# First backward heads of an attention block's gradient kernel: Wo products by batch with sums on TensorE, broadcasts moved, dV halves between V products

## Chip, cores and metric

The kernel runs on one core of one Trainium2 chip. The metric is the device time in microseconds, the median of three runs. Engines are named as in the profile: PE (TensorE), DVE (VectorE), ACT (ScalarE), POOL (GpSimd), SP (SyncE, which here only issues DMAs). PEld is PE's load of the stationary operand.

## The reference, cut to what matters

One decode step (one query row) through an adaLN-modulated attention block with a K/V cache and an MLP block, and its gradient.

```python
q = (x @ wq).reshape(B, Sq, Hq, Dh)              # Hq = 32 heads, Dh = 192
scores = einsum('bhqd,bhkd->bhqk', q, k_cache) * Dh ** -0.5   # 8192 keys
p = softmax(scores)
o = einsum('bhqk,bhkd->bhqd', p, v_cache)
a = o.reshape(B, Sq, Hq * Dh) @ wo               # wo: 6144 x 640
...
_out, _vjp = jax.vjp(_f, A_x, A_k_cache, A_v_cache, A_wq, A_wo, B_w3, B_w4, c, w_mod)
_grads = _vjp(grad_out)
```

All arrays are bf16. The large outputs are the gradients of the two caches, each 32 x 8192 x 192. For one head, with dao the gradient of `a` (640 numbers): `do = wo_h . dao` (192 numbers), `dP = V . do` and `dV = p x do` for each key, `dS = p * (dP - c)` with `c = do . o`, and `dK = dS x q`, an outer product as dV is.

## The kernel before

**Tiling.** A head's K or V is 128 partitions x 64 keys x 192. It is handled in two halves of 32 keys per partition ([128, 32, 192] in bf16, 1536 KB). A forward pass goes over heads 0 to 31, the MLP and its gradient follow, and a backward pass goes over heads 31 to 0 (`HS`; step `i` works on head 31 - i). V is loaded again for the backward pass; of K only head 31's tiles are read there (`dq_last`), still in place.

**One backward step i**, for head `h` and the next head `nxt`:
- `bwd_mult(h, t)` for both halves: DVE multiplies V by do in place (L132), PE sums the 192 products of each key by 24 matmuls with an identity (L1004) into a PSUM bank of 64 x 8 columns, `dP_ps`. The V slot is then free.
- `bwd_pf(nxt)`: p of the next head, on ACT as f32 (`PF`), on DVE as pairs in bf16 (`P2h`).
- `bwd_dv(nxt, t)`: an outer product of p and do in a store buffer; 20 of the 32 keys by ACT (L1009, one instruction per key), 12 by one DVE instruction (L987), then the store on SP's queue (L1012).
- `hook(i)` for the first ten steps (below).
- jobs that go with the step (rows of dWo and others, by ACT, stored from POOL's queue).
- `bwd_ds(h)`: DVE sums dP's 8 columns (L1030) and forms dS. For head 31, `dq_last` follows: 128 matmuls of K with dS.
- `bwd_dk(h, t)`: two outer products on DVE (L987), each stored on SP's queue (L1039).

Engines run in the order in which the program is written (`pin_order` ties PE, DVE and ACT to it), and SP's queue issues in that order too: a DMA whose condition is not met holds those behind it.

**Buffers.** dV and dK share a few tiles of 1536 KB (`big_tile`; tags 0 to 4 in a fixed order), so an outer product waits until an earlier store from its tile has landed. V has six slots. `ring_load` issues the next loads of a fixed list (`ring`) as far as the slot's last content is in `freed`; V loads go to SP's queue. The list also has Wo's rows in batches of two or three head pairs (`BATCHES`), loaded by `load_wo` from POOL's queue into one such slot.

**do of a head pair.** For the first pair it comes from PE. For the others, `bwd_ttr` (L921) multiplies 640 columns of Wo by dao in place and sums them, one DVE instruction for each of a pair's three blocks of 128 rows, 42 in the hooks 1 to 9 and three in hook 0. `ttrs` spreads a batch over two hooks, five blocks in the first and four in the second. After the batch, `fins` calls `fin_do` (to bf16), `fin_c` (c of these heads; a column sum on PE) and `fin_dq_mm` (up to 24 f32 matmuls for dq, read by `fin_dq` in the next step). `bwd_dob(hp)` broadcasts do and q of a pair over the partitions: three matmuls each, and a copy each by ACT (`pair_bc`, L191 and L195). It is called at the start of each odd step for the pair that the next head opens.

Of the kernel before, what the change touches and what calls it, by code (L numbers as in the profile page):

```python
# [12 lines left out]
AX = mybir.AxisListType  # L13
# [7 lines left out]
def kernel(  # L21
# [26 lines left out]
    nc = tc.nc  # L48
# [16 lines left out]
    P = 128  # L65
    D = A_x.shape[-1]
# [27 lines left out]
    def bank(tag, bufs=1, name=None, n=512):  # L94
        return psum[0].tile([P, n], FP32, tag=tag, name=name or "ps_" + tag, bufs=bufs)

    def bank_s(name):
        return bank("s", 2, name)
# [4 lines left out]
    ident_bf = const.tile([P, P], BF16, name="ident_bf")  # L103
# [24 lines left out]
    def ccol(n, name, dtype=FP32):  # L128
        return const.tile([P, n], dtype, name=name)

    def mul(out, a, b):
        nc.vector.tensor_tensor(out=out, in0=a, in1=b, op=ALU.mult)  # L132
# [459 lines left out]
    for i in range(1, HQ):  # L592
        c, p, pp = 2 <= i < HQ, 0 <= i - 1 < HQ, 0 <= i - 2 < HQ
        n = i + 1 < HQ
# [137 lines left out]
    HS = list(range(HQ - 1, -1, -1))  # L732
    PS = list(range(HH - 1, -1, -1))
    V_b = {HS[0]: st[HS[0]]["V"], HS[1]: {1: st[HS[1]]["V"][1]}}
    wo_src = {(PS[k], cc): st[2 * PS[k] + 1]["wo"][:, cc, :] for k in range(2) for cc in range(3)}
    BATCHES = [(2, 3, 4), (5, 6, 7), (8, 9, 10), (11, 12, 13), (14, 15)]
    ring = []
    for i in range(1, HQ):
        ring += [("v", HS[i], t) for t in range(2) if (i, t) != (1, 1)]
        if i % 2 == 1 and 0 < i // 2 < len(BATCHES):  # L740
            ring.append(("w", i // 2, 0))
# [4 lines left out]
    def ring_slot(n):  # L746
        return (3, 4, 5, 2, 0, 1)[n % NR]

    def ring_load():
        while ring_n[0] < len(ring) and (ring_n[0] < 3 or ring_key(ring_n[0] - NR) in freed):  # L750
            n = ring_n[0]
            kind, k, t = ring[n]
            slot = ring_slot(n)
            pool = bv if slot > 2 else fv
            ring_n[0] += 1
            if kind == "v":
                V_b.setdefault(k, {})[t] = load_v(pool, k, t, slot, ldq if n >= 3 else nc.sync)
            else:
                load_wo(k, pool.tile([P, JH, DH], BF16, name="V_sb", tag=f"v{slot}"))

    def load_wo(k, tl):
        lo, n = PS[BATCHES[k][-1]], len(BATCHES[k])
        tl = tl.rearrange("p j d -> p (j d)")[:, 0 : 3 * n * D].rearrange("p (c r) -> p c r", r=D)
        nc.gpsimd.dma_start(out=tl, in_=wo_v[:, 3 * lo : 3 * (lo + n), :])
        for hp in range(lo, lo + n):
            for cc in range(3):
                wo_src[hp, cc] = tl[:, 3 * (hp - lo) + cc, :]

    def ring_key(n):
        return ring[n] if n >= 0 else (("v", HS[0], 0), ("v", HS[0], 1), ("v", HS[1], 1))[n]  # L770
# [17 lines left out]
    def bwd_pf(h):  # L788
        bwd_pf_act(h)
        bwd_pf_dve(h)  # L790
# [26 lines left out]
    u = ccol(NFC, "u")  # L817
# [97 lines left out]
    dmod_bf = ccol(NMC, "dmod_bf", BF16)  # L915

    dof = ccol(NQC, "dof")
    r3_all = ccol(NQC, "r3_all")

    def bwd_ttr(hp, cc):  # L920
        nc.vector.tensor_tensor_reduce(out=wo_src[hp, cc], in0=wo_src[hp, cc], in1=dao_bc, scale=1.0, scalar=0.0, op0=ALU.mult, op1=ALU.add, accum_out=dof[:, 3 * hp + cc : 3 * hp + cc + 1])  # L921

    def fin_do(lo, n):
        sl = slice(3 * lo, 3 * (lo + n))
        dve_copy(do_bf[:, sl], dof[:, sl])

    def fin_c(lo, n):
        sl = slice(3 * lo, 3 * (lo + n))
        dve_copy(do_f[:, sl], do_bf[:, sl])
        pc = bsm.tile([P, 9], FP32, name="pc")[:, 0 : 3 * n]  # L930
        mul(pc, do_f[:, sl], o_col_f[:, sl])
        pc2 = bsm.tile([P, 6], FP32, name="pc2")[:, 0 : 2 * n]
        stt(pc2[:, 0 : 2 * n : 2], pc[:, 1 : 3 * n : 3], mask_lo[:, 0:1], pc[:, 0 : 3 * n : 3], ALU.mult, ALU.add)
        stt(pc2[:, 1 : 2 * n : 2], pc[:, 1 : 3 * n : 3], mask_hi[:, 0:1], pc[:, 2 : 3 * n : 3], ALU.mult, ALU.add)
        return col_sums(pc2, 2 * n, "c_ps")
# [22 lines left out]
    def dq_last(h):  # L958
        for t in range(2):
            sum_rows(dql_ps, 0, K_st[h, t], [bst[h]["dS2"][:, j, 0:1] for j in range(t * JH, (t + 1) * JH)], h, False, t == 1)  # L960
# [18 lines left out]
    def bwd_dob(hp):  # L979
        do_pb[hp] = pair_bc(bsm, do_bf, hp, "do_pb")  # L980
        q_pb[hp] = pair_bc(bsm, q_bf, hp, "q_pb")
# [41 lines left out]
    def bwd_dv(h, t):  # L1023
        o = big_tile("dV")
        bwd_dv_act(o, h, t)
        bwd_dv_dve(o, h, t)

    def bwd_ds(h):
        dP = bsm.tile([P, J], FP32, name="dP")
        nc.vector.reduce_sum(out=dP, in_=bst[h]["dP_ps"], axis=AX.X)  # L1030
        dS2 = bsm.tile([P, J, 2], BF16, name="dS2")
        stt(dS2, dP[:, :, None].to_broadcast([P, J, 2]), c_bc[:, h : h + 1], bst[h]["P2h"], ALU.subtract, ALU.mult)
        bst[h]["dS2"] = dS2
# [118 lines left out]
    NPH = 10  # L1152
# [20 lines left out]
    J2[NPH + 8].append(job_x0)  # L1173
    J2[NPH + 14].append(job_c)

    ttrs = {i: [] for i in range(NPH)}
    ttrs[0] = [(PS[1], cc) for cc in range(3)]
    fins = {}
    for b, ks in enumerate(BATCHES):
        units = [(PS[k], cc) for k in ks for cc in range(3)]  # L1180
        i = 1 + 2 * b
        ttrs[i] = units[0:5] if i + 1 < NPH else units
        if i + 1 < NPH:
            ttrs[i + 1] = units[5:]
        fins[min(i + 1, NPH - 1)] = (PS[ks[-1]], len(ks), b)
    dq, cps = {}, {}

    def hook(i):
        for u in ttrs[i]:
            bwd_ttr(*u)  # L1190
        if i == 0:
            fin_do(PS[1], 1)
            cps[i] = (PS[1], 1, fin_c(PS[1], 1))
        if i in fins:
            lo, n, b = fins[i]
            if b > 0:
                freed.add(("w", b, 0))
                ring_load()
            fin_do(lo, n)
            cps[i] = (lo, n, fin_c(lo, n))  # L1200
            dq[i] = (lo, n, fin_dq_mm(lo, n))
        if i == 3:
            dq[i] = (PS[1], 2, fin_dq_mm(PS[1], 2))
# [27 lines left out]
    dao_bc = late.tile([P, D], BF16, name="dao_bc")  # L1231
    bcast_dao()
    mid_mm()
    AHEAD = 2 * NPH
    for i in range(HQ):
        h, nxt = HS[i], HS[i + 1] if i + 1 < HQ else None
        if i % 2 == 1 and nxt is not None:
            bwd_dob(nxt // 2)
        for f in J0[i]:
            f()  # L1240
        if i <= AHEAD:
            for t in range(2):
                bwd_mult(h, t, 2 if i == 0 else 1)
                if i == t == 0:
                    ring_load()
                    c_first = fin_c(PS[0], 1)
        ring_load()
        if i - 1 in dq:
            fin_dq(*dq.pop(i - 1))
        if i == 0:  # L1250
            fin_c_copy(PS[0], 1, c_first)
        if nxt is not None:
            if i > 0:
                bwd_pf(nxt)
            for t in range(0 if i > 0 else 1, 2):
                bwd_dv(nxt, t)
        if i < NPH:
            hook(i)
        if i == 3:
            bcast_cols(du_bf, 0, NFC, du_bc, act_copy)  # L1260
        for f in J1[i]:
            f()
        bwd_ds(h)
        if i == 0:
            dq_last(h)
        if i >= AHEAD and nxt is not None:
            for t in range(2):
                bwd_mult(nxt, t)
        bwd_dk(h, 0)
        bwd_dk(h, 1)  # L1270
        if i in cps:
            fin_c_copy(*cps.pop(i))
        if i == 1:
            mid_cols()
            job_mid()
            dve_copy(dmod_bf[:, 2 * NDC : 6 * NDC], dmod_c[:, 2 * NDC : 6 * NDC])
        if i == NPH - 1:
            fin_dq(*dq.pop(i))
            mm_cm.__exit__(None, None, None)
            for nm, b in (("in", 1), ("out", 4), ("bc", 1)):  # L1280
                side_cm.append(tc.tile_pool(name="side" + nm, bufs=b, side="right", reuse_waits="tile"))
                side[nm] = side_cm[-1].__enter__()
        for f in J2[i]:
            f()
        if i == I_SIDE:
            while side_cm:
                side_cm.pop().__exit__(None, None, None)
            xt = ctx.enter_context(tc.tile_pool(name="xt", bufs=1, side="right", reuse_waits="tile"))
            for k in "xy":
                tail_tiles[k] = (xt, "xt" + k)  # L1290
            for n in range(len(ring) - NR, len(ring)):
                slot = ring_slot(n)
                tail_tiles[f"v{n - len(ring) + NR}"] = (bv if slot > 2 else fv, f"v{slot}")
            big_order[:] = tail_list(big_order[0:5] + ["x", "y"])
# [31 lines left out]
```

## Time and profile before

| | |
|---|---|
| median of 3 runs | 1379.54 us (1379.42 to 1380.29) |
| profiled execution, its own time | 1379.59 us |
| its span | 1377.8 us |
| granted TensorE clock, mean | 0.78 |
| DVE busy | 1070.5 us (78%) |
| ACT busy | 946.8 us (69%) |
| PE busy | 860.8 us (62%) |
| bytes moved by DMA | 569.26 MB (341.51 read, 225.91 written in HBM) |
| backward steps | from about 575 us on |

A slice of the page is 34.4 us. A row of a group gives the engine's line, what it writes and reads, how often, its busy time and mean duration, and behind the bar the engine's idle time before it with what ended most of it. In a table of windows each engine has its busy time in the window and a count of instructions. "SPq" is the DMA issue on SP's queue; its start is the moment at which it no longer waits.

### The profile page before, as it was taken

The numbers are of one execution on the slowest core, as the hardware profiler recorded it, in microseconds if no ns is written. First come the engines' busy times: TensorE is split into PE (matmuls) and PEld (weight loads), VectorE is DVE, ScalarE is ACT, GpSimd is POOL, SyncE is SP. The second block draws the span as 40 slices with busy tenths as digits, with TensorE's granted clock in tenths as the row PEclk, the third lists the DMA queues.
The fourth block names the chain that finished last, engine by engine and source line by source line (L and its number), as shares of the span: only waits on it lengthen the run. The fifth ranks groups of instructions, "written<-read, shape, count | busy, mean of one in ns | idle before, by whom it ended". The sixth has DMA issues, their size and how long they took to land.

```text
span 1377.8 us, 28365 instructions
## 1 busy us (share of the span) xinstructions
PE 860.8 (62%) x11655; PEld 675.9 (49%) x11655; DVE 1070.5 (78%) x1273; ACT 946.8 (69%) x2586; POOL 21.5 (2%) x33
## 2 busy tenths in 40 slices
PE   3799999999999999748545653443344325324440
PEld 3577777777777777736434542322223223213330
DVE  3588787888788787899988986965868669679792
ACT  1388777887778785866676676766767676767770
POOL 0000000000000000000000000000000000000000
PEclk9899999999999999666666665666666767656665
DMA  9999999999999999899999999999999999999997
GB/s 392 416 417 418 420 418 421 414 419 418 405 421 419 403 420 387 337 367 413 419 418 419 427 429 425 425 427 423 426 426 423 428 422 415 425 425 422 428 428 319
DMA packets 71758, 569.26 MB, mean 413 GB/s; under 512 B 6796, under 2 KB 14476, under 8 KB 31436
## 3 DMA queue, kind: packets, MB, share of 16 engines
q1 hardware_dynamic: 67934, 550.73, 96.1%
q0 software_dynamic: 3664, 16.71, 3.0%
q8 instruction: 91, 1.49, 0.4%
q14 instruction: 39, 0.32, 0.1%
q10 hardware_dynamic: 30, 0.00, 0.0%
HBM read 341.51 MB, written 225.91 MB: 412 GB/s over the span
## 4 chain that ended last, share of the span: by engine, by line
DMA 37%; DVE 29%; PE 22%; ACT 6%; SPq 3%; issue 2%; DVEq 0%; ACTq 0%
DMA out_dram<-dV 24%; DVE prod L132 9%; PE ps_a L432 8%; DVE dK L987 5%; DVE V_sb L132 5%; DMA out_dram<-dK 4%; PE S_ps L372 4%; DMA V_sb<-in_A_v_cache_dram 3%; DMA K_sb<-in_A_k_cache_dram 3%; ACT dV L1009 3%; PE ps_b L443 3%; PE kb_ps L449 2%; DVE dV L987 2%; DVE V_sb L921 2%; DMA out_dram<-dw 2%
## 5 line engine op out<-in xcount | busy, mean ns | idle before, releaser
L1009 ACT ACTIVATE dV<-do_pb,PF 128x192 bf16<-128x192 bf16 x1246 | 435.8, 440 | 141.9 <-DMA out_dram<-dV 101.3
L1004 PE MATMUL dP_ps<-V_sb,ident_bf 128*128 128x256 bf16 (+1 forms) x1584 | 233.3, 322 | 212.0 <-DVE V_sb L132 212.0
L407 ACT ACTIVATE EK<-K_sb,E_f 128x192 bf16<-128x192 bf16 x992 | 351.1, 442 | 4.3 <-PE kb_ps L302 2.9
L1004 PEld LDWEIGHTS <-ident_bf 128*128 128x128 bf16 x1584 | 180.9, 117 | 264.2 <-issue 138.9
L987 DVE TENSOR_TENSOR dK<-dS,q_pb 128x6144 bf16<-128x6144 bf16 x64 | 212.9, 3354 | 26.2 <-DMA out_dram<-dK 15.6
L132 DVE TENSOR_TENSOR prod<-K_sb,q_pb 128x6144 bf16<-128x6144 bf16 x64 | 214.4, 3349 | 4.1 <-DMA K_sb<-in_A_k_cache_dram 4.1
L132 DVE TENSOR_TENSOR V_sb<-V_sb,do_pb 128x6144 bf16<-128x6144 bf16 (+1 forms) x66 | 212.0, 3253 | 0.0
L432 PE MATMUL ps_a<-EK,V_sb 128*128 128x193 bf16 x1984 | 195.1, 251 | 1.3 <-DMA V_sb<-in_A_v_cache_dram 1.3
L432 PEld LDWEIGHTS <-V_sb 128*128 128x128 bf16 x1984 | 167.8, 100 | 19.3 <-issue 12.7
L987 DVE TENSOR_TENSOR dV<-P2h,do_pb 128x2304 bf16<-128x2304 bf16 (+2 forms) x67 | 89.5, 1354 | 111.3 <-DMA out_dram<-dV 106.8
L414 DVE TENSOR_TENSOR EK<-K_sb,P2h 128x1536 bf16<-128x1536 bf16 x124 | 117.5, 948 | 0.0
L372 PE MATMUL S_ps<-prod,ident_bf 64*64 64x256 bf16 x3072 | 101.3, 280 | 11.5 <-DVE prod L132 11.5
L443 PE MATMUL ps_b<-EK,V_sb 128*64 128x193 bf16 x1984 | 107.7, 250 | 0.0
L372 PEld LDWEIGHTS <-ident_bf 64*64 64x64 bf16 x3072 | 86.5, 110 | 31.0 <-issue 26.9
L443 PEld LDWEIGHTS <-V_sb 128*64 128x64 bf16 x1984 | 80.8, 110 | 19.6 <-issue 15.9
L393 ACT ACTIVATE E_f<-sm_ps,negm 128x64 f32<-128x64 f32 x31 | 9.8, 315 | 103.9 <-DVE negm L391 103.9
L376 DVE TENSOR_REDUCE S<-S_ps 128x128 f32<-128x1024 f32 x32 | 39.2, 1224 | 47.7 <-PE S_ps L372 47.6
L1115 PEld LDWEIGHTS <-ident_bf 128*128 128x128 bf16 x112 | 15.2, 136 | 123.8 <-issue 122.9
L449 PE MATMUL kb_ps<-EK,hot_bf 128*32 128x384 bf16 x992 | 63.5, 333 | 0.0
L1115 PE MATMUL js_ps<-wq,ident_bf 128*128 128x480 bf16 x64 | 23.8, 557 | 53.3 <-DVE wq L132 53.3
L1115 PE MATMUL js_ps<-wm,ident_bf 128*128 128x400 bf16 x48 | 14.9, 494 | 48.7 <-DVE wm L132 48.7
L195 ACT CAST do_pb<-bc_ps 128x384 bf16<-128x384 f32 x15 | 7.1, 474 | 52.0 <-PE bc_ps L191 52.0
(259 smaller groups left out, 758.5 us busy)
## 6 DMA issues: line engine op xcount, KB each, us to landing
V_sb<-in_A_v_cache_dram SPq DMA_DIRECT2D x125, 1536.0 KB, 14.8
K_sb<-in_A_k_cache_dram SPq DMA_DIRECT2D x64, 1536.0 KB, 14.2
out_dram<-dK SPq DMA_DIRECT2D x64, 1536.0 KB, 24.0
out_dram<-dV SPq DMA_DIRECT2D x61, 1536.0 KB, 22.3
wq<-in_A_wq_dram SPq DMA_DIRECT2D x3, 2560.0 KB, 31.4
wo_t<-in_A_wo_dram SPq DMA_DIRECT2D x16, 480.0 KB, 14.3
out_dram<-dwo POOLq DMA_DIRECT2D x16, 480.0 KB, 8.9
wq<-in_A_wq_dram SPq DMA_DIRECT2D x4, 1920.0 KB, 23.7
```

The costliest lines, as they stand in the source:

```text
L132: nc.vector.tensor_tensor(out=out, in0=a, in1=b, op=ALU.mult)
L372: nc.tensor.matmul(st["S_ps"][c0 : c0 + 64, r, t * JH : (t + 1) * JH, :], lhsT=ident_bf[64 * r : 64 * r + 64, 64 * r : 64 * r + 64], rhs=p ...
L376: nc.vector.reduce_sum(out=st["S2"], in_=st["S_ps"], axis=AX.X)
L407: nc.scalar.activation(out=st["EK"][q][:, jj, 0:DH], in_=K_st[h, t][:, r * JQ + jj, :], func=ACT.Copy, scale=st["E_f"][:, j : j + 1])
L414: nc.vector.tensor_tensor(out=EK[:, NA:JQ, 0:DH].rearrange("p j (d r) -> p j d r", r=2), in0=K_st[h, t][:, r * JQ + NA : (r + 1) * JQ, :]. ...
L432: nc.tensor.matmul(st["A_ps"][:, 0:n], lhsT=V_sb[:, r * JQ + jj, a0:a1], rhs=EK[:, jj, 0:n], start=(q == 0 and jj == 0), stop=(q == 3 and ...
L443: nc.tensor.matmul(st["B_ps"][g : g + 64, 0:n], lhsT=V_sb[:, r * JQ + jj, b0:b1], rhs=EK[:, jj, 0:n], start=(q == 0 and jj < 2), stop=(q = ...
L449: nc.tensor.matmul(kb_ps[g : g + 32, 0 : 2 * DH], lhsT=hot_bf[:, HQ - 1 - h : 2 * HQ - 1 - h], rhs=EK[:, jj : jj + 2, 0:DH], start=(h == 0 ...
L987: nc.vector.tensor_tensor(out=o.rearrange("p j (d r) -> p j d r", r=2), in0=pairs[:, :, None, :].to_broadcast([P, n, NP2, 2]), in1=vec.rea ...
L1004: nc.tensor.matmul(bst[h]["dP_ps"][:, t * JH + r : t * JH + r + n, :], lhsT=ident_bf, rhs=V_sb[:, :, k * DS : (k + 1) * DS], start=(k == 0 ...
L1009: nc.scalar.activation(out=o[:, jj, :], in_=vec_of(do_pb, h), func=ACT.Copy, scale=bst[h]["PF"][:, t * JH + jj : t * JH + jj + 1])
L1115: nc.tensor.matmul(ps[:, 0 : NDC * W].rearrange("p (i w) -> p i w", w=W), lhsT=ident_bf, rhs=w[:, :, k * W : (k + 1) * W], start=(k == 0), ...
```

## The change

- The 42 Wo products of the hooks 1 to 9 become one DVE product per batch (`bwd_wo_mult`, at the odd steps), over the whole tile of 6 or 9 blocks with dao repeated. PE then sums the products of a block from 640 to 32 columns by 20 matmuls with the identity into a PSUM bank of the tag that `dP_ps` uses, and DVE sums the 32 in `bwd_wo_red`, at the next even step (for the last batch in the same step). The batch's slot counts as free after the matmuls, a step earlier than before.
- `bwd_dob` moves from the start of the odd steps into the hook of the even step before, ahead of `fin_c` and `fin_dq_mm`; from step 11 on it stays where it was. In step 0 it stands in hook 0, ahead of `fin_c`.
- In step 0, `bwd_ds` and `dq_last` move ahead of the hook.
- In steps 1 to 3 (`SPLIT`), `bwd_pf` comes first, and each `bwd_dv` half follows one `bwd_mult` half.
- `ring_load` moves behind `bwd_dv` in all steps (the one inside step 0's first half stays).

```diff
+    wo_b = {}
+    WS = 32
...
+        wo_b[k] = tl
         nc.gpsimd.dma_start(out=tl, in_=wo_v[:, 3 * lo : 3 * (lo + n), :])
-        for hp in range(lo, lo + n):
-            for cc in range(3):
-                wo_src[hp, cc] = tl[:, 3 * (hp - lo) + cc, :]
...
+    def bwd_wo_mult(b):
+        lo, n = PS[BATCHES[b][-1]], len(BATCHES[b])
+        w = wo_b.pop(b)
+        mul(w, w, dao_bc[:, None, :].to_broadcast([P, 3 * n, D]))
+        ps = bank_s("dof_ps")[:, 0 : 3 * n * WS].rearrange("p (c w) -> p c w", w=WS)
+        for k in range(D // WS):
+            nc.tensor.matmul(ps, lhsT=ident_bf, rhs=w[:, :, k * WS : (k + 1) * WS], start=(k == 0), stop=(k == D // WS - 1))
+        dof_ps[b] = (ps, lo, n)
+
+    def bwd_wo_red(b):
+        ps, lo, n = dof_ps.pop(b)
+        nc.vector.reduce_sum(out=dof[:, 3 * lo : 3 * (lo + n)], in_=ps, axis=AX.X)
...
+    fins = {min(2 + 2 * b, NPH - 1): b for b in range(len(BATCHES))}
...
     def hook(i):
-        for u in ttrs[i]:
-            bwd_ttr(*u)
         if i == 0:
+            for u in wo_first:
+                bwd_ttr(*u)
             fin_do(PS[1], 1)
+            bwd_dob(PS[1])
             cps[i] = (PS[1], 1, fin_c(PS[1], 1))
-        if i in fins:
-            lo, n, b = fins[i]
+            return
+        if i % 2 == 1:
+            b = (i - 1) // 2
+            bwd_wo_mult(b)
             if b > 0:
                 freed.add(("w", b, 0))
                 ring_load()
+        if i in fins:
+            b = fins[i]
+            lo, n = PS[BATCHES[b][-1]], len(BATCHES[b])
+            bwd_wo_red(b)
             fin_do(lo, n)
+            if i % 2 == 0:
+                bwd_dob(HS[i + 2] // 2)
             cps[i] = (lo, n, fin_c(lo, n))
             dq[i] = (lo, n, fin_dq_mm(lo, n))
...
+    SPLIT = range(1, 4)
     for i in range(HQ):
         h, nxt = HS[i], HS[i + 1] if i + 1 < HQ else None
-        if i % 2 == 1 and nxt is not None:
+        if i % 2 == 1 and i > NPH and nxt is not None:
             bwd_dob(nxt // 2)
         for f in J0[i]:
             f()
         if i <= AHEAD:
+            if i in SPLIT:
+                bwd_pf(nxt)
             for t in range(2):
                 bwd_mult(h, t, 2 if i == 0 else 1)
                 if i == t == 0:
                     ring_load()
                     c_first = fin_c(PS[0], 1)
-        ring_load()
+                if i in SPLIT:
+                    bwd_dv(nxt, t)
...
-        if nxt is not None:
+        if nxt is not None and i not in SPLIT:
             if i > 0:
                 bwd_pf(nxt)
             for t in range(0 if i > 0 else 1, 2):
                 bwd_dv(nxt, t)
+        ring_load()
+        if i == 0:
+            bwd_ds(h)
+            dq_last(h)
         if i < NPH:
             hook(i)
...
-        bwd_ds(h)
-        if i == 0:
-            dq_last(h)
+        if i > 0:
+            bwd_ds(h)
```

More of the change, by code (lines that the diff above doesn't have):

```diff
@@ L917 @@
     dof = ccol(NQC, "dof")
+    dof_ps = {}
     r3_all = ccol(NQC, "r3_all")
@@ L1174 @@
     J2[NPH + 14].append(job_c)
[L1176 to L1185, printed above, removed]
+    wo_first = [(PS[1], cc) for cc in range(3)]
+    fins = {min(2 + 2 * b, NPH - 1): b for b in range(len(BATCHES))}
     dq, cps = {}, {}
     def hook(i):
-        for u in ttrs[i]:
-            bwd_ttr(*u)
         if i == 0:
+            for u in wo_first:
+                bwd_ttr(*u)
             fin_do(PS[1], 1)
+            bwd_dob(PS[1])
             cps[i] = (PS[1], 1, fin_c(PS[1], 1))
-        if i in fins:
-            lo, n, b = fins[i]
+            return
+        if i % 2 == 1:
+            b = (i - 1) // 2
+            bwd_wo_mult(b)
             if b > 0:
```

## The prediction

> **What bounds the kernel now.** I read the page's slices first (busy tenths and GB/s), then a table of windows, then the DMA queue's own timeline beside those of ACT and PE, then the groups of the rows that change.
>
> The slices (section 2 of the page: 40 slices of 34.4 us):
>
> ```profile
> DVE  3588787888788787899988986965868669679792
> DMA  9999999999999999899999999999999999999997
> GB/s 392 416 417 418 420 418 421 414 419 418 405 421 419 403 420 387 337 367 413 419 418 419 427 429 425 425 427 423 426 426 423 428 422 415 425 425 422 428 428 319
> ```
>
> DVE is the busiest compute engine, but the 16 DMA engines are busy nearly throughout. The only deep dip inside is 337 GB/s in the 17th slice (551 to 585 us) and 367 in the next (585 to 620). The windows say where bytes are missing (columns: window, length, busy time of PE, PEld, DVE, ACT, POOL with counts, clock, DMA share, GB/s):
>
> ```profile
> 560.00:581.00 21.00, 13.37 (x226) 12.53 (x222) 17.58 (x39) 17.50 (x49) 1.14 (x1) 0.59 0.82 316
> 581.00:612.00 31.00, 16.82 (x242) 14.08 (x239) 30.62 (x38) 21.94 (x60) 1.80 (x2) 0.71 0.91 340
> 612.00:700.00 88.00, 56.02 (x342) 46.52 (x343) 85.88 (x133) 63.16 (x171) 4.38 (x5) 0.66 1.01 416
> 700.00:1350.00 650.00, 269.51 (x1650) 199.07 (x1649) 506.35 (x371) 444.24 (x1149) 13.07 (x17) 0.65 1.01 425
> 1350.00:1378.00 28.00, 0.00 (x0) 0.00 (x0) 1.45 (x1) 0.00 (x0) 0.00 (x0) 0.50 0.68 290
> ```
>
> From 700 us on the DMA carries 425 GB/s without a gap, and after 1350 us only queued stores drain: the end is "all bytes moved", and bytes do not change. A microsecond is won only where bytes are missing against 425 GB/s: 31 x (1 - 340/425) = 6.2 us in 581 to 612, 88 x (1 - 416/425) = 1.9 us in 612 to 700, none later. The 5.4 us in 560 to 581 lie before the code that changes. So the ceiling is 8.1 us, whatever DVE saves. In 612 to 700 DVE is 98% busy too, but the DMA is full beside it.
>
> Finer windows put 2.7 us of the 6.2 in one hole:
>
> ```profile
> 602.00:604.00 2.00, 2.00 (x11) 1.45 (x10) 2.00 (x2) 2.00 (x7) 0.00 (x0) 0.50 0.33 131
> 604.00:606.00 2.00, 2.00 (x20) 1.77 (x19) 2.00 (x6) 2.00 (x7) 0.00 (x0) 0.99 0.71 147
> 608.00:610.00 2.00, 0.00 (x0) 0.00 (x0) 1.93 (x5) 2.00 (x5) 0.00 (x0) 1.00 0.88 233
> ```
>
> The queue's timeline says why (start, length, issue):
>
> ```profile
> 581.43 3.27 SPq L330 DMA_DIRECT2D V_sb<-in_A_v_cache_dram  x2
> 585.44 0.34 SPq L1012 DMA_DIRECT2D out_dram<-dV  x1
> 591.75 3.60 SPq L1039 DMA_DIRECT2D out_dram<-dK  x2
> 603.68 0.34 SPq L330 DMA_DIRECT2D V_sb<-in_A_v_cache_dram  x1
> 604.12 4.69 SPq L1012 DMA_DIRECT2D out_dram<-dV  x2
> ```
>
> Five transfers of 1536 KB, about 3.7 us each at 425 GB/s, are issued from 581.43 on and are through at 602.4 us. The next issue is the V load at 603.68, which waits for PE to finish dP of head 30's first half; behind it on SP stands the first dV store of head 29, though its own data (DVE at 603.1, ACT at 601.5) are ready. In the windows the rate rises about 1 us after an issue into an empty queue.
>
> **The change in i = 0.** ds moves ahead of hook(0). It needs PE's dP, done at 584.33, which the three L921 instructions covered till now; so DVE waits 0.2 us, and dK starts at about 588.7 instead of 588.36. dq_last on PE (588.38 to 592.2 now) moves to about 585.4 to 589.3. Behind it come the broadcasts of do and q of pair 14, now in hook(0): ACT copied do_pb at 592.72 after an idle 7.31 us, and now can at about 589.9. So ACT begins head 29's dV at 591.7 instead of 594.53: 2.8 us earlier. ring_load moves behind the dV: the second V load issues after the dV store, at 585.8 instead of 584.36. The DMA then has read, write, read, write where it had read, read, write.
>
> **i = 1 to 3 (SPLIT).** DVE runs product, dV, product, dV. With dK's two tiles done at 595.4: P2h 0.22, product 3.35, dV 1.35, hence 600.4; ACT's 20 (13.93/40 = 0.348 each) end at 598.7. The first dV store issues at 600.4 instead of 604.12 and its data can flow at 601.4, before the queue is empty at 602.4: the hole closes. The second is ready at 605.7 (ACT), then the V load right behind, its slot being free since about 603. The first dV occupies the DMA to 606.1, the second flows from 606.7: a gap of up to 0.6 us. What is queued behind SP's longer waits are V loads for heads three later: loads issued around 606 are used near 660, and land 16.4 us after issue in the median.
>
> **Wo products.** Removed: 42 L921 instructions in hooks 1 to 9.
>
> ```profile
> L132 DVE TENSOR_TENSOR V_sb<-V_sb,do_pb 128x6144 bf16<-128x6144 bf16 x22 | 72.8, 3350 | 0.0
> L921 DVE CUSTOM_DVE_ANT_0 V_sb<-V_sb,dao_bc 128x640 bf16<-128x640 bf16 x42 | 32.0, 819 | 0.0
> L1030 DVE TENSOR_REDUCE dP<-dP_ps 128x64 f32<-128x512 f32 x12 | 8.2, 688 | 0.2
> ```
>
> One follows the other after 0.745 us: 42 x 0.745 = 31.3 us. Added: four products of 5760 elements and one of 3840 at 3.35/6144 each (3.14 and 2.09 us), and five sums from PSUM of 288 or 192 columns (688 ns for 512 columns, 1224 for 1024, so about 0.45 and 0.35): 16.8 us. DVE saves 14.5 us on paper. PE gets 20 matmuls per batch; 48 of 256 columns took 8.1 us, so 20 of 288 about 3.8 us (7 if each counted its whole 335 ns), before dq's matmuls; PE is 64% busy there. In i = 2, DVE waits some 1.2 us for dP, whose second half now starts a dV later; in i = 9 it waits some 4 us for PE's sum. All of this lies in stretches where the DMA is at 416 to 425 GB/s, so I book nothing for it except an earlier, deeper queue in 612 to 700. If the queue were dry there, these waits would cost 5 us.
>
> **Broadcasts and the load order elsewhere.** At even i the broadcasts stand ahead of dq's matmuls (8.5 us on PE in i = 2): ACT's idle 10.14 us before do_pb at 641.74 goes, and dV stores of odd heads come some 7 us earlier (650.6 and 657.5 now). The Wo slot is freed a head sooner, so V loads of head 25 start sooner; from i = 4 on V loads stand behind dV stores. Bytes are the same.
>
> **The sum**, against the profiled execution's 1379.59 us (span 1377.8 and 1.8 around it; the median 1379.54 is the same):
> - hole in 602 to 606: 1.38 + 1.31 = -2.69
> - the 0.90 us missing in 608 to 610, where reads turn to writes just after the hole: half of it, -0.45 (0 to -0.9), since one such turn stays
> - 612 to 700: half of 1.9, -0.9 (0 to -1.9); part is the Wo load's small packets, which stay
> - the added read/write turn in 586 to 595: a turn from reads to writes cost 0.35 + 0.56 = 0.91 us in 588 to 592 (350 and 307 GB/s); one more each way, 0 to 1.8. Later, with a deep queue, turns show no loss, so I take +0.7
> - gap before the second dV: +0.3 (0 to 0.6)
>
> Together -3.0: **1376.5 us**; the terms' ends give -5.5 to -0.3. A rule of the Trainium skill puts a DMA at a fixed 2.0 us plus bytes/436e9 (DMA: Bandwidth & Descriptors, section Anatomy of one DMA — SWDGE (gpsimd) path), with no term for direction. By it the turn would cost nothing; the trace's 350 and 307 GB/s with a full queue speak against it.
>
> **Rivals.**
> A. Turns are free when the next issue is already queued. Then -2.69 - 0.9 - 0.9 + 0.3 = -4.2: 1375.4 us. For it: 700 to 1350 holds 425 GB/s with two turns per head. Against: 588 to 592. Chance 0.18. (The rule above would make this one happen.)
> B. The hole moves instead of closing: the broadcast comes no earlier, because PE reaches it behind dq_last only when ACT is busy or DVE late. Then ACT ends its second 20 at 608.5, and the V load, until now at 603.68, stands behind that store; the queue is empty from 606 to 609.5. About 3 us lost for 2.7 won, some regained later: 1379 us. For it: V loads behind a wait of ACT. Against: ACT's 7.31 us of idle time before do_pb. With cases in which the turns take most of the gain: chance 0.20.
> C. Slower: from i = 4 on V loads wait on SP behind a dV store that itself waits for a free store buffer. After a buffer lands, the refill takes 20 x 0.348 + 1 = 8.0 us. Five buffers leave up to four stores (14.7 us) to carry it; if only two lie ahead (7.4 us), the DMA is dry 0.6 us per head, some 14 us over 23 heads: 1391 us. Against: DVE and ACT wait for landed stores now (16 us of dV in 700 to 860), with 22 us from a store's issue to landing. Chance 0.10. The Trainium skill (Perfetto Trace Analysis, section DMA Optimizations) advises separate issuing engines for inputs and outputs; the change ties loads closer to stores on one queue, which is this case. No run here shows the price.
>
> **How the numbers follow.** Forecast 0.52, A 0.18, B 0.20, C 0.10. About 0.2% (2.8 us) is what a measurement of this kernel can tell from no change: the forecast lies close to that bound at 1376.8. I put 0.6 of its chance beyond it. Faster: 0.31 + 0.18, so 0.50; within: 0.21 + 0.20, so 0.40; slower 0.10. The forecast's own range is 1374.5 to 1378.8; with A and B the range is 1373.6 to 1380.8, which leaves out C.
>
> **What would show it.** Right: the first dV store of head 29 issued at about 600.4 us and no two-microsecond window below 250 GB/s in 600 to 610; do_pb of pair 14 copied near 590; 612 to 700 above 416 GB/s; 700 on at 425; DVE's busy time down by some 14 us with the span down by 3. Wrong: a hole between 606 and 610 (B); the order read, write, read, write without a dip (A); a rate below 420 from 700 on (C), or the span falling with DVE's saving, which would mean that bytes were not the bound.

## The result, and the profile after

The changed kernel takes 1388.41 us (median; 1387.75 to 1391.25) where the kernel before took 1379.6 beside it: 1.0068 of it [1.0055, 1.0081], 9 us slower. The forecast was 1376.5 with 1373.6 to 1380.8. The profiled execution took 1388.55 us, its span is 1386.8.

The page's slices of the changed kernel:

```profile
DMA  9999999999999999899999999999999999999997
GB/s 392 417 419 420 417 420 419 417 419 418 406 421 417 406 420 386 337 403 424 423 417 423 419 421 428 417 407 423 404 417 409 408 425 396 414 417 418 418 429 310
```

The dip in the 18th slice has mostly gone, as forecast (403 where it was 367). But from the 26th slice on, where nearly every slice was above 420, values of 396 to 418 are common, and the line of DMA tenths shows nothing of it. The table of windows (columns as before the change: window, length, PE, PEld, DVE, ACT, POOL, clock, DMA share, GB/s):

```profile
560.00:581.00 21.00, 13.26 (x213) 12.51 (x211) 17.07 (x39) 17.47 (x49) 1.15 (x1) 0.59 0.83 319
581.00:612.00 31.00, 18.59 (x254) 15.23 (x253) 30.49 (x29) 25.44 (x71) 1.82 (x2) 0.72 0.97 381
612.00:700.00 88.00, 57.90 (x382) 48.18 (x382) 81.33 (x100) 64.48 (x172) 5.19 (x6) 0.72 1.01 421
700.00:1350.00 650.00, 275.97 (x1690) 204.17 (x1690) 489.13 (x333) 436.93 (x1135) 12.29 (x16) 0.66 1.01 416
```

Against 425 GB/s, 581 to 612 wins 31 x 41/425 = 3.0 us (381 for 340) and 612 to 700 wins 88 x 5/425 = 1.0 us. Then 700 to 1350 runs at 416 instead of 425, at the same DMA share of 1.01: it moves 270.56 MB where it moved 275.99, and 5.43 MB at 425 GB/s are 12.8 us. 12.8 - 4.0 = 8.8 us, and the span grew by 9.0. So everything is in this table: the start won 4.0 us where the forecast had 3.0, and a loss for which the sum had no term lies in the long stretch behind it.

The start, first on SP's queue (start, length, issue), then on ACT and DVE:

```profile
581.01 0.34 SPq L330 DMA_DIRECT2D V_sb<-in_A_v_cache_dram  x1
584.95 0.33 SPq L1026 DMA_DIRECT2D out_dram<-dV  x1
585.37 0.38 SPq L330 DMA_DIRECT2D V_sb<-in_A_v_cache_dram  x1
591.49 3.60 SPq L1053 DMA_DIRECT2D out_dram<-dK  x2
599.53 5.14 SPq L1026 DMA_DIRECT2D out_dram<-dV  x2
604.76 0.39 SPq L330 DMA_DIRECT2D V_sb<-in_A_v_cache_dram  x1
```

```profile
589.25 0.48 ACT L195 CAST do_pb<-bc_ps 128x384 bf16<-128x384 f32 x1 [4.33 <-PE bc_ps L191]
...
598.12 1.35 DVE L1001 TENSOR_TENSOR dV<-P2h,do_pb 128x2304 bf16<-128x2304 bf16 x1
```

do_pb of pair 14 is copied at 589.25 (forecast: near 590) and head 29's first dV store is issued at 599.53 (600.4). The hole is closed:

```profile
590.00:592.00 2.00, 0.37 (x2) 0.31 (x3) 2.00 (x2) 1.97 (x7) 0.00 (x0) 0.50 0.93 356
...
602.00:604.00 2.00, 2.00 (x13) 1.44 (x11) 2.00 (x3) 2.00 (x7) 0.00 (x0) 0.58 1.01 430
604.00:606.00 2.00, 2.00 (x20) 1.79 (x19) 2.00 (x2) 2.00 (x4) 0.00 (x0) 1.00 1.00 420
...
608.00:610.00 2.00, 1.74 (x15) 1.16 (x12) 1.97 (x2) 2.00 (x7) 0.61 (x1) 1.00 1.09 338
610.00:612.00 2.00, 0.00 (x0) 0.00 (x0) 2.00 (x2) 2.00 (x7) 0.00 (x0) 1.00 0.97 368
```

430 and 420 GB/s stand where 131 and 147 stood, and 338 where 233 stood; but 610 to 612 fell from 436 to 368. The groups that answer for DVE, first of the kernel before, then of the changed one:

```profile
L987 DVE TENSOR_TENSOR dK<-dS,q_pb 128x6144 bf16<-128x6144 bf16 x64 | 212.9, 3354 | 26.2 <-DMA out_dram<-dK 15.6
L987 DVE TENSOR_TENSOR dV<-P2h,do_pb 128x2304 bf16<-128x2304 bf16 (+2 forms) x67 | 89.5, 1354 | 111.3 <-DMA out_dram<-dV 106.8
```

```profile
L1001 DVE TENSOR_TENSOR dK<-dS,q_pb 128x6144 bf16<-128x6144 bf16 x64 | 213.8, 3356 | 96.1 <-DMA out_dram<-dK 95.4
L1001 DVE TENSOR_TENSOR dV<-P2h,do_pb 128x2304 bf16<-128x2304 bf16 (+2 forms) x67 | 89.1, 1353 | 39.1 <-DMA out_dram<-dV 28.4
L132 DVE TENSOR_TENSOR V_sb<-V_sb,dao_bc 128x5760 bf16<-128x5760 bf16 x4 | 12.6, 3152 | 0.0
L935 DVE TENSOR_REDUCE dof<-dof_ps 128x9 f32<-128x288 f32 x4 | 1.8, 452 | 0.0
```

DVE's busy time fell from 1070.5 to 1056.1 us, by 14.4 (forecast 14.5). None of it became time: DVE's idle time in the span went from 307.3 to 330.7 us, by the 14.4 us and the 9.0 us of longer span. The wait for a buffer's last store moved from dV's products (111.3 us of idle time before them, now 39.1) to dK's (26.2, now 96.1).

### The profile page after: what moved, and what is told of

Same layout as the page of the kernel before. It is cut to its first block, busy times and chain, and to the rows that moved or that the text cites. A ratio compares the mean times of both kernels' runs of the same rounds, so it can differ in the third digit from the quotient of the medians.

```text
span 1386.8 us, 28498 instructions
## 1 busy us (share of the span) xinstructions
PE 871.3 (63%) x11755; PEld 684.2 (49%) x11755; DVE 1056.1 (76%) x1199; ACT 944.8 (68%) x2586; POOL 21.5 (2%) x33
## 3 DMA queue, kind: packets, MB, share of 16 engines
q1 hardware_dynamic: 67934, 550.73, 96.1%
## 5 line engine op out<-in xcount | busy, mean ns | idle before, releaser
L1001 DVE TENSOR_TENSOR dK<-dS,q_pb 128x6144 bf16<-128x6144 bf16 x64 | 213.8, 3356 | 96.1 <-DMA out_dram<-dK 95.4
L1001 DVE TENSOR_TENSOR dV<-P2h,do_pb 128x2304 bf16<-128x2304 bf16 (+2 forms) x67 | 89.1, 1353 | 39.1 <-DMA out_dram<-dV 28.4
L372 PE MATMUL S_ps<-prod,ident_bf 64*64 64x256 bf16 x3072 | 101.3, 280 | 11.3 <-DVE prod L132 11.3
L1068 ACT ACTIVATE wq_o<-wq_bc,ha_f 128x1536 bf16<-128x1536 bf16 x12 | 18.7, 1568 | 39.5 <-DMA out_dram<-wq_o 39.5
L191 PE MATMUL bc_ps<-ident_bf,dq_bf 128*128 128x128 bf16 x48 | 6.4, 304 | 54.3 <-ACT do_pb L195 53.1
L1068 ACT ACTIVATE wm_o<-wm_bc,sc_f 128x1280 bf16<-128x1280 bf16 x9 | 12.2, 1357 | 36.8 <-DMA out_dram<-wm_o 36.6
## 6 DMA issues: line engine op xcount, KB each, us to landing
wo_t<-in_A_wo_dram SPq DMA_DIRECT2D x16, 480.0 KB, 14.5
```

The lines of the kernel that those rows point to most:

```text
L372: nc.tensor.matmul(st["S_ps"][c0 : c0 + 64, r, t * JH : (t + 1) * JH, :], lhsT=ident_bf[64 * r : 64 * r + 64, 64 * r : 64 * r + 64], rhs=p ...
L1001: nc.vector.tensor_tensor(out=o.rearrange("p j (d r) -> p j d r", r=2), in0=pairs[:, :, None, :].to_broadcast([P, n, NP2, 2]), in1=vec.rea ...
L1068: nc.scalar.activation(out=out, in_=in_, func=ACT.Copy, scale=col)
```

## The experiments

**Undo only the order of loads, or do only that.** e1 puts the loads ahead of the dV stores again from step 4 on; e2 is the kernel before with nothing but the loads moved behind dV.

```
e1, against the changed kernel:
+        if i > 3:
+            ring_load()          # ahead of fin_dq and dV
e2, against the kernel before:
-        ring_load()              # ahead of fin_dq and dV
...
+        ring_load()              # behind dV
```

> The changed kernel, but from step 4 on ring_load stands ahead of the dV again, as in the kernel before. Theory L (the load order: V loads behind dV stores lower the rate from 700 us on; the profile after has 416 GB/s there against 425, worth 650 x 9/425 = 13.8 us, against 3.0 and 1.0 us won in 581 to 612 and 612 to 700): 1375 to 1377 us, 424 GB/s or more in 700 to 1350. Theory W (the rate is lost by the Wo products, the broadcasts or the new pace of DVE, not by the load order): 1387 to 1390 us, 416 GB/s.

> The kernel before, with ring_load behind the dV in all steps and nothing else of the change. Theory L: 1388 to 1394 us, 415 to 418 GB/s in 700 to 1350, hole in 602 to 606 still there. Theory W: 1379 to 1381 us, 425 GB/s.

e1: 1377.06 us, 0.9973 [0.9962, 0.9985] of the kernel before. e2: 1392.89, 1.0086 [1.0071, 1.0101]. The two windows of each that decide, e1 first:

```profile
581.00:612.00 31.00, 18.93 (x273) 16.12 (x270) 29.91 (x29) 25.93 (x73) 1.82 (x2) 0.76 0.96 378
...
700.00:1350.00 650.00, 279.20 (x1696) 205.36 (x1693) 498.42 (x338) 440.29 (x1139) 13.06 (x17) 0.67 1.01 424
```

```profile
581.00:612.00 31.00, 16.80 (x255) 14.60 (x253) 30.62 (x38) 23.04 (x63) 1.33 (x2) 0.72 0.92 345
...
700.00:1350.00 650.00, 263.55 (x1619) 195.56 (x1619) 495.13 (x367) 443.49 (x1151) 13.05 (x17) 0.65 1.01 416
```

The move alone costs 13.0 us and gives the 416 GB/s; without it the rest of the change wins 2.9 us and 700 to 1350 is at 424. This is shown both ways, and theory W falls. e1 beats both kernels.

**From which step on, and how far behind.** e3 is e1 with `if i > 9`. x1 puts the loads of steps 4 on between the two dV halves; x2 puts them behind both dK stores.

> The changed kernel, with ring_load ahead of the dV from step 10 on only; steps 4 to 9 keep the changed order. Theory L, with the loss where the rate is low (after: 419 to 421 GB/s in 700 to 800, 411 to 414 in 900 to 1100): about 2 us of the loss stay, 1377 to 1379 us. Theory W: 1387 to 1390 us.

> The changed kernel, with ring_load between the two dV halves from step 4 on (queue order dV, V, V, dV, dK, dK). Theory A (addresses: V loads are slowed when they stand right behind stores into dV's array): V still follows a dV store, 1386 to 1390 us, rate in 700 to 1350 below 419. Theory C (compute: V loads are slow where they land while DVE's product, PE's sums and ACT's dV all run; the mean packet of 12288 bytes took 503 ns in that state after, 467 before, 460 elsewhere): loads land some 4 to 7 us earlier, so another loss, 1378 to 1388 us.

> The changed kernel, with ring_load behind both dK stores from step 4 on (queue order dV, dV, dK, dK, V, V; the order of the transfers is that of the kernel before, the issues come where they come now). Theory A: 1375 to 1379 us, 424 GB/s. Theory C: V loads land some 8 us later than after, 1378 to 1388 us.

e3: 1378.57 us, 0.9988 [0.9979, 0.9998]; so most of the loss arises from step 10 on, as expected. x1: 1379.41, 0.9994 [0.9983, 1.0005]. x2: 1381.17, 1.0007 [0.9996, 1.0018]. The loss is not one that grows with the distance from the old place: x2's loads stand two stores further back than the change's and lose 4 us against e1, where the change loses 11. Theory A falls in both: it had x1 at 1386 us or more, and x2 at 1379 or less with 424 GB/s (421 in 700 to 1350). Theory C's ranges hold both times, but they are wide; it is looked at below.

**What it is not: POOL's stores, or the array that is written.** e4 issues the dWo and dw4 rows from SP instead of POOL. x4 (the changed kernel) and x5 (the kernel before) let dK and dV change places in the two large outputs.

> The changed kernel, with the stores of dWo and of the rows of dw4 issued on SP's queue in program order instead of POOL's. Theory P (the slow stretches begin where a POOL store of dWo runs beside the second dV store just before the V loads: 971 to 975, 1030 to 1034, 1087 to 1092 us; the 16 DMA engines get out of step there): those stretches go, 1376 to 1380 us. Theory L without P: 1386 to 1390 us.

> The changed kernel, with the stores of dV going to dK's output array and those of dK to dV's (the two outputs change places; all else is the same). Theory A: the V loads now follow stores into the other array: 1375 to 1380 us. Theory C: 1387 to 1390 us as after.

> The kernel before, with the output arrays of dV and dK exchanged in the same way. Theory A: V loads, which follow dK's stores, now follow stores into the array that slows them: 1388 to 1394 us. Theory C: 1379 to 1381 us as before.

e4: 1389.59 us, 1.0064 [1.0049, 1.0079]. x4: 1391.56, 1.0081 [1.0051, 1.0111]. x5: 1379.42, 1.0002 [0.9991, 1.0013]. Theory P falls with e4 and theory A again with x4 and x5: neither POOL's stores nor the array has to do with it. x4 (two runs) lies 1.6 us above what C gave. Which head is read and written side by side, and so the place inside the arrays, was not varied.

**Where the lost bytes are.** The 12288-byte packets, which make up the large transfers, can be averaged from the trace, with 460 ns as their usual duration; to tell loads from stores, they are counted off in the order of the queue. In 700 to 1350 us their mean is 463.6 ns before the change and 472.3 after it; e1 463.8, e2 472.8, e3 464.5, x1 465.2, x2 464.5, e4 471.6, x4 473.5, x5 463.7. It follows the times except in x2, whose 4 us these packets do not explain. The 18,932 packets of the changed kernel at 8.7 ns more, over 16 engines, are 10.3 of the 12.8 us; a share of 1.008 where it was 1.011 is 1.8 us of the rest.

The longer time does not fall on all transfers: dK's packets stay at 462 (461 before), V's go from 468 to some 482, dV's from 462 to 472. From step 11 to 19 it is the V loads of the odd steps, with the end of the second dV store just ahead of them, that stand out: some 505 to 550 ns for the first, 490 to 520 for the second, and 460 to 467 in the even steps, though there too the loads stand right behind the second dV store. In steps 11, 13, 15 and 17 packets lengthen while stores alone are moved, 3.5 to 4.2 us before the first packet of the loads starts (from 918.5 us on in step 11, where that packet starts at 922.0). So, as far as the packets' starts tell, it is not the turn from stores to loads that begins it. Two windows of the changed kernel, around the loads of step 13 (odd) and step 14:

```profile
976.00:988.00 12.00, 7.20 (x44) 5.39 (x44) 11.28 (x10) 10.45 (x31) 0.00 (x0) 0.58 0.99 367
1011.00:1020.00 9.00, 3.36 (x28) 2.65 (x27) 6.01 (x3) 9.00 (x28) 0.00 (x0) 0.82 1.01 421
```

367 GB/s at a share of 0.99. The queue is not dry there: what is issued and not yet moved is mostly 4.5 to 7.5 MB, and over the whole stretch packets are no slower where less is queued (some 465 ns at 3.0 to 4.5 MB, 478 at 4.5 to 6.0). Theory C's state does not make the difference either: while DVE's product of V, PE's sums and ACT's dV all ran, packets of V loads took 493 to 509 ns in the slow orders (after, e2, y3, x4) and 463 to 466 in the fast ones (before, e1, g1, z5).

**What stands in the queue.** Steps 11 to 19 carry the jobs of wq and w_mod: every second step ends with a load for a job, and their row stores lie between the large ones. y1 (the changed kernel) and y2 (e1) have none of these jobs, y3 has all of them one step later, z1 has their row stores on POOL's queue, z2 has only their loads a step later.

```
y1, y2:  for g in range(0) / enumerate(())      # no add_outer, job_x0, job_c
y3:      add_outer(NPH + 2 * g, ...)  add_outer(NPH + 8 + 2 * k, ...)   # one step later
z1:      nc.gpsimd.dma_start(out=dram[i * P : (i + 1) * P, lo : lo + n], in_=o)
z2:      J2[at + 1].append(lambda: job_outer_load(name, view, lo, n))
```

> The changed kernel without the jobs of the outer products of wq and w_mod: their loads, products and stores are left out (out_4, out_9, and of x's and c's gradients the parts that need them). That is 12.8 MB less read and 12.8 MB less written, 60 us at 425 GB/s. In the changed kernel the slow stretches lie in steps 11 to 24, where these jobs run, at V loads ahead of which no wq load stands in the queue. Theory J (the loss needs these jobs' small transfers in the queue): 700 us on at 423 to 425 GB/s, V loads' packets at 460 to 470 ns, and no more than 4 us behind its partner below (loads ahead of the dV stores). Theory D (the pattern is one of the big stores and loads alone; a wq load only breaks it): the V loads are slow in all steps now, mean packets of V loads 490 ns or more, rate 416 GB/s or less, 10 to 25 us behind the partner.

> The partner: loads ahead of the dV stores from step 4 on, and the same jobs left out. Both theories: V loads' packets near 465 ns, 424 GB/s from 700 us on, and about 60 us below the 1377.1 us that this order takes with the jobs, so 1317 us.

> The changed kernel with all jobs of wq and w_mod one step later, so that their loads stand at the end of even steps instead of odd ones (the side buffers are given back a step later too). In the changed kernel V loads of odd steps 11 to 19 are slow (packets 491 to 552 ns), those of even steps, which have a wq load ahead of them, are not (460 to 465). Theory Q (what stands ahead of the stores in the queue decides): the slow V loads change to even steps. Theory T (the step's own parity decides: the buffer, or do's broadcasts on PE in odd steps): they stay in the odd steps. Either way the time stays near 1388 us (1386 to 1391).

> The changed kernel with the row stores of the outer products (wq_o, wm_o: five per job, 1536 or 1280 columns) issued from POOL's queue instead of SP's; loads as in the changed kernel. The loss without these jobs was 5 us instead of 11 (1317.7 against 1312.5). Theory S (the small stores in SP's queue make the V loads behind the next dV stores slow): V loads' packets in 860 to 1160 us at 470 ns or less, time 1380 to 1383. Theory W2 (the wq load decides, by standing ahead of the dV stores or not): V loads of odd steps 11 to 19 stay at 490 to 550 ns, 1387 to 1391 us.

> The changed kernel with only the wq and w_mod loads of these jobs a step later, at the end of even steps; their stores stay where they are. Theory S: the slow V loads stay in odd steps. Theory W2: they move to even steps, and the odd ones are at 460 to 470 ns. Time 1386 to 1391 us by both.

y1: 1317.74 us and y2: 1312.53 (4.5 us below what was expected of it, which no run explains), so 5.2 us between the two orders where 11.3 lie with the jobs (mean packets 467.4 and 463.8 ns). About half of the loss needs the jobs and half does not: both theories missed. y3: 1388.56, 1.0057 [1.0044, 1.0071], and the slow V loads now lie in the even steps (501 to 558 ns; 460 to 465 in the odd ones): Q holds and T falls. z2: they move to the even steps as well, mostly to the second load there, with the small stores left in place, as W2 said. But its time is 1399.33, 1.0147 [1.0133, 1.0161], 8 us above what was expected, for a reason of its own: the job's product waits for its load.

```profile
L132 DVE TENSOR_TENSOR wq<-wq,wq_bc 128x7680 bf16<-128x7680 bf16 x4 | 16.6, 4158 | 71.6 <-DMA wq<-in_A_wq_dram 71.6
```

In the changed kernel this group waits 0.0 us; z2's 1150 to 1280 us have a DMA share of 0.94 and 383 GB/s. z1: 1388.46, 1.0065 [1.0044, 1.0086]. The odd steps' V loads fall to some 460 to 500 ns and the mean to 468.8, but the time stays, as DMA shares of 0.99 with 408 GB/s appear in 1150 to 1280. S expected such packets, but a time of 1380 to 1383; W2 expected the time, but packets of 490 to 550 ns. So the load's place alone does not decide, and why the rate is low there is not shown.

**Loads from another queue.** In z3, POOL issues the V loads of the backward pass, and no V load stands behind a waiting store of dV or dK.

```
-    ldq = nc.sync
+    ldq = nc.gpsimd        # the wq and w_mod loads stay on nc.sync
```

> The changed kernel with all V loads of the backward pass issued from POOL's queue, so that no load stands behind a store that waits; the wq and w_mod loads stay on SP. Theory L (what costs 11 us is the loads' place behind dV stores on one queue): 1376 to 1380 us and 423 to 425 GB/s from 700 us on, unless what POOL does itself or its issue costs something (then up to 1385, with V loads late). If loads and stores mixed in another order always cost the same, whatever queue issues them: 1385 to 1391 us.

1392.2 us, 1.0099 [1.0083, 1.0116], with 413 GB/s from 700 us on:

```profile
700.00:1350.00 650.00, 263.00 (x1642) 196.69 (x1642) 473.98 (x327) 428.20 (x1108) 37.99 (x63) 0.66 1.00 413
```

The expectation of theory L fails, and the time lies 1 us above the other range. V's packets take 483 ns on this queue, as much as in the changed kernel (some 482), and POOL's own row stores land later, z3 first, then the changed kernel (the page's DMA issues; the last column is us from issue to landing):

```profile
out_dram<-dwo POOLq DMA_DIRECT2D x16, 480.0 KB, 21.1
```

```profile
out_dram<-dwo POOLq DMA_DIRECT2D x16, 480.0 KB, 9.5
```

The Trainium skill (Perfetto Trace Analysis, section DMA Optimizations) says that it may make sense to give inputs one issuing engine and outputs another. With POOL as that engine it did not help here; no other engine was tried.

**The prices of the start.** g1 is e1 without the split (dV behind both products in steps 1 to 3). z5 is e1 with the loads first in step 0 as well.

> Loads ahead of the dV stores from step 4 on, and dV behind both V products in steps 1 to 3 as before the change. It prices the split. The forecast's sum gave the hole in 602 to 606 us 2.7 us and the turn behind it 0.45: if that is right the time is 1377.1 + 3 = 1380 us and 581 to 612 falls from 378 GB/s to about 345. If the earlier broadcasts alone fill the hole, 1377 to 1378 us and 581 to 612 above 365 GB/s.

> Loads ahead of the dV stores from step 4 on (1377.1 us) and in step 0 as well, so that the DMA has two reads and then two writes there, as before the change. It prices the forecast's added turn between reads and writes: if that cost its +0.7 us (0 to 1.8), 1376.4 us (1375.3 to 1377.1) and some 382 GB/s or more in 581 to 612 instead of 378. If turns are free (rival A): 1377.1 and 378 GB/s.

g1: 1379.6 us, 0.9997 [0.9988, 1.0005], with 360 GB/s in 581 to 612 and the hole in its old place:

```profile
602.00:604.00 2.00, 2.00 (x12) 1.34 (x10) 1.97 (x4) 2.00 (x7) 0.00 (x0) 0.50 0.35 147
604.00:606.00 2.00, 2.00 (x14) 1.54 (x13) 2.00 (x3) 2.00 (x6) 0.00 (x0) 0.69 0.68 272
```

The split is worth 1379.6 - 1377.06 = 2.5 us, and the Wo products with the broadcasts, everything else that g1 has, are worth 0.3 us, less than can be told from nothing. z5: 1378.36, 0.9988 [0.9979, 0.9997], and 375 GB/s in 581 to 612: not faster than e1. The old order of step 0 gains nothing; z5 has 236 GB/s in 592 to 594, so it is no clean price of the turn. That is read better from e1, which has the changed order in step 0:

```profile
588.00:590.00 2.00, 2.00 (x76) 1.97 (x73) 1.86 (x10) 0.00 (x0) 0.00 (x0) 0.70 1.05 442
590.00:592.00 2.00, 1.65 (x24) 1.33 (x21) 2.00 (x1) 1.19 (x4) 0.00 (x0) 0.50 1.03 420
```

## Why the prediction was wrong

- **What bounds the kernel: right.** Bytes bound it before and after; 14.4 us less of DVE work became idle time.
- **Hole in 602 to 606, -2.69: right.** 430 and 420 GB/s instead of 131 and 147. g1 against e1 prices the split at 2.5 us.
- **608 to 610, -0.45: within its range.** 338 for 233 GB/s is 2 x 105/425 = 0.49 us, but 368 for 436 in 610 to 612 gives 0.32 of it back.
- **612 to 700, -0.9: right**, 1.0 us by 421 for 416.
- **The added turn, +0.7: not seen, and its price was misread.** 590 to 592 shows 356 GB/s where 307 stood, and 420 in e1. The bytes missing in 588 to 592 before the change lie inside the second V load, whose packets took 573 ns in the mean; the first packet of the dV store behind it starts at 591.5 us. Those missing in 608 to 610 lie inside the V load issued at 603.68 (673 ns; dV's first packet at 610.0). So what was priced as a turn from reads to writes was loads with long packets, the kind of loss that the sum left out behind 700 us. Rival A's step was the better one here, though the whole (381 GB/s, 3.0 us in 581 to 612) came out larger than the forecast's terms for it (-2.1 with the gap's +0.3).
- **Wo products: right.** 3.15 us for 3.14, sums of 0.45; nothing gained, as booked. DVE's wait for PE's sum in i = 9 was 1.9 us instead of some 4.
- **The step that failed: "from i = 4 on V loads stand behind dV stores. Bytes are the same", booked at nothing** and followed by "700 on at 425". It cost 11.3 us in the changed kernel (e1) and 13.0 alone (e2). With that term in place the sum had come out: e1, the change without it, is 2.9 us faster than the kernel before, against 3.0 forecast, in part by luck, as a turn that was not there stood against a larger gain in 581 to 612. The sum took "DMA busy without a gap" to mean a fixed rate. The rate depended on the order of the same transfers: 425 or 416 GB/s, both at a share of 1.01.
- **Rival C named the place and the size** (1391 us, loads behind dV stores from step 4 on), but not the mechanism: it had the DMA run dry 0.6 us per head. No dry queue was found; the packets themselves are longer. That it came near 1388.41 us is luck. Its chance of 0.10 rested on the argument that enough stores were queued, which is true and did not help.
- **What stays open** is why the packets are longer. Shown: the loads right behind the second dV store are hit, and the end of that store, where it begins, but not in every step, and hardly the loads between the halves (x1) or behind dK (x2); the hit steps change with the place of the jobs' load (y3, z2); part of it needs the jobs (y1), and their row stores bear on it too (z1). Excluded: POOL's stores, the output array, a dry queue, and what DVE, PE and ACT run at that moment as a cause by itself.

## What to carry to other kernels

When the DMA is full, "no byte changes" does not make a reordering of its queue free: price a change of the order by a run of that part alone, and read GB/s beside the DMA share, since the share stayed at 1.01 through a loss of 2%. Split a change into the part that closes a hole and the part that only comes along with it: here the split of dV won 2.5 us, and a line moved beside it lost 11. The best kernel of these runs keeps the change and puts the loads first again from step 4 on (1377.06 us).

## What the hardware showed beyond expectation

- One order of loads and stores on a queue that is never dry moved 2% fewer bytes per microsecond than another; packets of 12288 bytes rose from 460 ns to means of some 500 to 550 over stretches of some 12 us, beginning in stores ahead of the loads.
- The same V loads issued from POOL's queue took 483 ns per packet, no less than the some 482 of the changed kernel and more than e1's 468, and POOL's row stores then landed after 21.1 us instead of 9.5.
